# One PSUM bank per step in a Fourier mixing and gated feed-forward kernel: P, then Q added onto it

## The chip, the cores and the metric

The kernel runs on one core of one Trainium2 chip. The metric is the device time of one execution in microseconds (us). A profile of one execution gives, for every engine, when each instruction ran. The engines are TensorE (PE in the views, its weight loads PEld), VectorE (DVE), ScalarE (ACT), GpSimd (POOL) and SyncE (SP), which starts the transfers. Each engine works through its own list of instructions in order[...], so what an engine does late holds up everything behind it in its list. TensorE writes its results to PSUM[...]; the other engines read them from there.

## The reference, cut to what matters

```python
def _attn_ref(x):                       # x: (8, 3008, 256) float32
    X = np.fft.fft(x, axis=1)
    X = np.fft.fft(X, axis=2)
    return X.real

def _moe_ref(x, w_in, w_out):           # x: (24064, 256), w_in: (256, 2048), w_out: (2048, 256)
    h = x @ w_in
    g = h * (1.0 / (1.0 + np.exp(-1.702 * h)))
    return g @ w_out
```

A two-dimensional Fourier transform (its real part) of eight batches is followed by a feed-forward layer: a product, a sigmoid-gated activation, a product.

## The kernel before

The kernel uses symmetries of the real part. The last stage of the transform along the 256 columns is folded into `w_in`, and two rows of the input of the feed-forward layer come from the same two products, called P and Q here: one row has the hidden values P + Q, its mirror row P - Q + N, where N is a correction of rank one (`nb` times a column of `af2`).

The work is cut into 384 steps: 8 batches x 3 blocks x 2 halves x 8 pairs of 128 hidden features (`p`). Eight consecutive steps with the same block and half form a group; they add their output products onto the same banks. A step has 256 columns, in one of the six groups of each batch 225.

In every step the two products P and Q go into one bank each, `pa` and `pb`. ScalarE copies P to SBUF, VectorE makes P + Q, N - Q and P - Q + N (this last one in reversed order of columns), and one activation runs over both halves of `h`:

```python
def hidden(t):
    ...
    pa, pb = bank("pa"), bank("pb")                  # from a ring of four banks
    for ps, cs in ((pa, 0), (pb, 1)):
        for i in range(2):
            f = 2 * p + i
            halves(ps[:, i * 256:i * 256 + n], wcs[cs][:, f * 128:(f + 1) * 128], pq[:, cs, ks], start=True, stop=True)
    v = sp.tile([128, 512], F32, tag="v", name="v")
    nc.scalar.copy(two(v[:], n), two(pa[:], n))

def rows(t):
    ...
    nc.vector.tensor_tensor(two(h[:], n), two(v[:], n), two(pb[:], n), op=ALU.add)
    for i in range(2):
        f = 2 * p + i
        nc.vector.scalar_tensor_tensor(dif[:, i * 256:i * 256 + n], nb[:, ks], af2[:, f:f + 1],
                                       pb[:, i * 256:i * 256 + n], op0=ALU.mult, op1=ALU.subtract)
    ...                                              # h (second half, reversed) = pa + dif
def activate(t):
    g = free(ht[t][:], 0, [256, 4], [1, width(blk, hh)])
    nc.scalar.activation(g, g, ACTF.Gelu_apprx_sigmoid)
```

`halves` issues every product as two matmuls with 64 columns of weights each; each appears in the profile as two matmuls. A step thus has 8 x 2 matmuls for P and Q and, for the output, 7 x 2 x 2 = 28: the second product is done with a scheme of seven products in place of eight (Strassen's, in Winograd's form), except in the first eight steps. Its sums of `h` are made by GpSimd (`s1`, `s3`) and VectorE (`s2`, `s4`) in `sums`, and `product(t)` adds the seven products onto four banks. After the eighth step of a group `combine` puts the seven sums together on VectorE, transposes them and starts the stores:

```python
def combine(t):                                      # n columns; nothing unless p is the last
    ...
    for out_, i0, i1, how in ((u2, c1, m6, ALU.add), (c11, c1, m2, ALU.add), (u3, u2, m7, ALU.add),
                              (u2, u2, m5, ALU.add), (c12, u2, m3, ALU.add), (c22, u3, m5, ALU.add),
                              (c21, u3, m4, ALU.subtract)):
        nc.vector.tensor_tensor(out_, i0, i1, op=how)
    ...
    for half in range(2):
        turned(half, c[:, 2 * half:])                # one transpose of 128 x 512, then the stores
```

The main loop, with the order in which each engine gets its work:

```python
    for t in range(n + LAG):                         # LAG = 3
        if t < n:
            hidden(t)
        ...
        if t >= LAG:
            product(t - LAG)
        ...
        if 0 < t <= n:
            activate(t - 1)
            sums(t - 1, nc.gpsimd)
        sums(t - 2, nc.vector)
        if t < n:
            rows(t)
        if t >= LAG:
            combine(t - LAG)
        for fn, args in extra.get(t, ()):            # work of the next batch and block
            fn(*args)
```

The work in `extra` is the transform of the next batch and block: `fold1` on GpSimd (eight pieces, in every second step from the 7th of a batch on), `mix1` (16 products and two copies by ScalarE, in the steps 10, 14, 18 and 22 of a batch; in the first batch three steps later), `stage2` (products and four transposes by VectorE, in the steps 8, 24 and 40 of a batch).

Of the kernel before, what the change touches and what calls it, by code (L numbers as in the profile page):

```python
# [27 lines left out]
F32 = mybir.dt.float32  # L28
# [83 lines left out]
def kernel(ctx: ExitStack, tc, x, w_in, w_out, tab1, tab2, out):  # L112
# [13 lines left out]
    sp = ctx.enter_context(tc.tile_pool(name="sp", bufs=2, space=SB))  # L126
    op = ctx.enter_context(tc.tile_pool(name="op", bufs=2, space=SB))
    cv = ctx.enter_context(tc.tile_pool(name="cv", bufs=1, space=SB))
    psm = ctx.enter_context(tc.tile_pool(name="psm", bufs=4, space=PS))
    pso = ctx.enter_context(tc.tile_pool(name="pso", bufs=1, space=PS))  # L130
    ctx.enter_context(tc.manual_schedule())

    Xr = [nc.dram_tensor(f"Xr{b}", (NA, NJ, D), F32, kind="Internal").ap() for b in range(B)]
# [16 lines left out]

        return w[rows, jj * NM:jj * NM + 64]

    def bank(name):
        return psm.tile([128, 512], F32, tag="mm", name=name)

# [299 lines left out]

    NP = NF // 2
    steps = [(b, blk, hh, p) for b in range(B) for blk in range(NBLK) for hh in range(2) for p in range(NP)]
    vb, ht, st, pot, ot = {}, {}, {}, {}, {}  # L460

    def width(blk, hh):

        return 225 if (blk, hh) == (0, 1) else 256

    def two(ap, n):
        return free(ap, 0, [256, 2], [1, n])

    def halves(out, lhs, rhs, **how):
        for c0 in (0, 64):  # L470
            nc.tensor.matmul(out[c0:c0 + 64], lhsT=lhs[:, c0:c0 + 64], rhs=rhs, **how)  # L471

    def hidden(t):

        b, blk, hh, p = steps[t]
        n = width(blk, hh)
        pq, ks = pqt[b, blk], slice(hh * 256, hh * 256 + n)
        pa, pb = bank("pa"), bank("pb")
        for ps, cs in ((pa, 0), (pb, 1)):
            for i in range(2):  # L480
                f = 2 * p + i
                halves(ps[:, i * 256:i * 256 + n], wcs[cs][:, f * 128:(f + 1) * 128], pq[:, cs, ks], start=True, stop=True)
        v = sp.tile([128, 512], F32, tag="v", name="v")

        nc.scalar.copy(two(v[:], n), two(pa[:], n))  # L485
        vb[t] = v, pa, pb

    def rows(t):
        b, blk, hh, p = steps[t]
        n = width(blk, hh)  # L490
        nb, ks = nbt[b, blk], slice(hh * 256, hh * 256 + n)
        v, pa, pb = vb.pop(t)
        h = ht[t] = hp.tile([128, 2, 2, 256], F32, tag="h", name="h")
        dif = sp.tile([128, 512], F32, tag="dif", name="dif")
        nc.vector.tensor_tensor(two(h[:], n), two(v[:], n), two(pb[:], n), op=ALU.add)  # L495
        for i in range(2):
            f = 2 * p + i
            nc.vector.scalar_tensor_tensor(dif[:, i * 256:i * 256 + n], nb[:, ks], af2[:, f:f + 1],  # L498
                                           pb[:, i * 256:i * 256 + n], op0=ALU.mult, op1=ALU.subtract)

        full, rest = divmod(n, RUN)
        for at, blocks, m in ((0, full, RUN), (full * RUN, 1, rest)):
            if m:
                ins = [free(x[:], at, [256, 2], [RUN, blocks], [1, m]) for x in (pa, dif)]
                nc.vector.tensor_tensor(free(h[:], 512 + at + m - 1, [256, 2], [RUN, blocks], [-1, m]), *ins, op=ALU.add)  # L505

    def activate(t):
        b, blk, hh, p = steps[t]
        g = free(ht[t][:], 0, [256, 4], [1, width(blk, hh)])
        nc.scalar.activation(g, g, ACTF.Gelu_apprx_sigmoid)  # L510

    def sums(t, eng):

        if not NP <= t < len(steps):
            return
        h, n = ht[t], width(*steps[t][1:3])
        a11, a12, a21, a22 = h[:, 0, 0, :n], h[:, 0, 1, :n], h[:, 1, 0, :n], h[:, 1, 1, :n]
        if eng is nc.gpsimd:
            st[t] = sp.tile([128, 4, 256], F32, tag="s", bufs=3, name="s")
        s1, s2, s3, s4 = (st[t][:, q, :n] for q in range(4))  # L520
        if eng is nc.gpsimd:
            eng.tensor_tensor(s1, a21, a22, op=ALU.add)  # L522
            eng.tensor_tensor(s3, a11, a21, op=ALU.subtract)  # L523
        else:
            eng.tensor_tensor(s2, s1, a11, op=ALU.subtract)  # L525
            eng.tensor_tensor(s4, a12, s2, op=ALU.subtract)  # L526

    def product(t):

        b, blk, hh, p = steps[t]  # L530
        n = width(blk, hh)
        if p == 0:
            for q in range(4):
                pot[q] = pso.tile([128, 2, 256], F32, tag=f"o{q}", name=f"po{q}")
        h = ht.pop(t)
        if t < NP:

            plan = [(half, dh, wo[:, p, 2 * f + dh, :], h[:, half, f, :n], f)
                    for half in range(2) for dh in range(2) for f in range(2)]
        else:  # L540
            s = st.pop(t)
            plan = ((0, 0, wo[:, p, 0, :], h[:, 0, 0, :n], 0), (0, 1, wt[:, p, 1, :], s[:, 1, :n], 0),
                    (1, 0, wo[:, p, 2, :], h[:, 0, 1, :n], 0), (1, 1, wt[:, p, 2, :], s[:, 2, :n], 0),
                    (2, 0, wt[:, p, 0, :], s[:, 0, :n], 0), (2, 1, wo[:, p, 3, :], s[:, 3, :n], 0),
                    (3, 0, wt[:, p, 3, :], h[:, 1, 1, :n], 0))

        if t == len(steps) - 2:
            pot["plan"] = plan
            return
        if t == len(steps) - 1:  # L550
            plan = [it for two_ in zip(pot.pop("plan"), plan) for it in two_]

        for q, i, lhs, rhs, f in plan:
            halves(pot[q][:, i, :n], lhs, rhs, start=(p == 0 and i == 0 and f == 0), stop=(p == NP - 1), skip_group_check=True)
        if p < NP - 1 or t < NP:
            return
        c1 = pot["c"] = op.tile([128, 256], F32, tag="u0", bufs=1, name="u0")
        nc.scalar.copy(c1[:, :n], pot[0][:, 0, :n])  # L558

    def combine(t):  # L560

        b, blk, hh, p = steps[t]
        if p < NP - 1:
            return
        n = width(blk, hh)
        o = op.tile([128, 4, 256], F32, tag="os", name="os")

        def turned(half, src):

            nc.vector.transpose(free(o[:], half * 512, [32, 2], [64, 8], [1, 32]), free(src, 0, [256, 2], [32, 8], [1, 32]))  # L570
            store(b, blk, hh, o, half)

        if t < NP:
            for half in range(2):
                turned(half, pot[half][:])
            return
        c = cv.tile([128, 4, 256], F32, tag="m", bufs=2, name="c")
        if n < 256:
            nc.gpsimd.memset(c[:, :, n:], 0.0)
        (_, m6), (m2, m7), (m5, m3), (m4, _) = ((pot[q][:, 0, :n], pot[q][:, 1, :n]) for q in range(4))  # L580
        u2, u3 = (op.tile([128, 256], F32, tag=f"u{q}", bufs=1, name=f"u{q}")[:, :n] for q in (1, 2))
        c1 = pot["c"][:, :n]
        c11, c12, c21, c22 = (c[:, q, :n] for q in range(4))
        for out_, i0, i1, how in ((u2, c1, m6, ALU.add), (c11, c1, m2, ALU.add), (u3, u2, m7, ALU.add),
                                  (u2, u2, m5, ALU.add), (c12, u2, m3, ALU.add), (c22, u3, m5, ALU.add),
                                  (c21, u3, m4, ALU.subtract)):
            nc.vector.tensor_tensor(out_, i0, i1, op=how)  # L587
            if t == len(steps) - 1:
                if out_ is c12:
                    turned(0, c[:])  # L590
                elif out_ is c22 or out_ is c21:
                    i = int(out_ is c22)
                    nc.vector.transpose(free(o[:], 512 + 32 * i, [64, 8], [1, 32]), free(c[:], (2 + i) * 256, [32, 8], [1, 32]))
        if t == len(steps) - 1:
            store(b, blk, hh, o, 1)
            return
        for half in range(2):
            turned(half, c[:, 2 * half:])

    def store(b, blk, hh, o, half):  # L600

# [118 lines left out]
    def at(t, fn, *args):  # L720
        extra.setdefault(t, []).append((fn, args))
# [16 lines left out]
    at(4, rotate, 0, 4, NG)  # L738
    for i in range(NCK):
        at(7 + i, differences, i)  # L740
    for b in range(B):
        t0 = b * NBLK * NF
        late = 0 if b else 3
# [16 lines left out]
                at(t0 + blk * NF + 12, nyquist, *nxt)  # L760

    for t in range(n + LAG):
        if t < n:
            hidden(t)
        if t == 0:
            low_up(in2)
            nyquist(0, 0)
            low_down(in2)
        if t in rows_at:
            first_row(rows_at[t])  # L770
        if t >= LAG:
            product(t - LAG)
        if t in early:
            fold_w(early[t])

        if 0 < t <= n:
            activate(t - 1)
            sums(t - 1, nc.gpsimd)
        sums(t - 2, nc.vector)
        if t < n:  # L780
            rows(t)
        if t >= LAG:
            combine(t - LAG)
        for fn, args in extra.get(t, ()):
            fn(*args)

# [27 lines left out]
```

## Time and profile before

| | us |
|---|---|
| median of three runs | 1920.59 (1920.14 to 1921.92) |
| span of the profiled execution | 1919.2 |
| PE busy | 1907.5 (99%) |
| PEld busy | 1284.4 (67%) |
| DVE busy | 1409.3 (73%) |
| ACT busy | 674.7 (35%) |
| POOL busy | 768.2 (40%) |

The first part of the profile page gives the busy time of each engine as a share of the span. Matmuls overlap one another, so that a busy PE alone does not tell that it works at its peak; for that one looks at the distance between the starts of its instructions in the timeline. The groups give, for the instructions of one line and shape, their count, their busy time, the mean duration of one, and the idle time of the engine just before them with what ended it. The chain of waits follows the last instruction back to what released it, again and again, and gives shares of the span by engine.

### The profile page before, as it was taken

To read this page: it belongs to the slowest core of one execution; us is meant where nothing else is said; L and a number is where in the kernel's file an instruction comes from. 1 tells how busy PE (TensorE), PEld (TensorE's weight loads), DVE (VectorE), ACT (ScalarE), POOL (GpSimd) and SP (SyncE) were. 2 spreads that over 40 slices of the span, in tenths; PEclk is the share of its full clock that TensorE was granted. 3 is DMA by queue.
4 is the path that set the end of the run, shared out by engine and by line. 5 is a ranking of instruction groups with operands and counts; after the bars stand their busy time and mean duration, and the time that the engine had idled before them with its cause. 6 is when DMAs were issued, how large, how long until landed. Compare 5 with 4: busy or idle time off the path is not lost.

```text
span 1919.2 us, 46708 instructions
## 1 busy us (share of the span) xinstructions
PE 1907.5 (99%) x19184; PEld 1284.4 (67%) x19184; DVE 1409.3 (73%) x2937; ACT 674.7 (35%) x932; POOL 768.2 (40%) x1057
## 2 busy tenths in 40 slices
PE   9999999999999999999999999999999999999998
PEld 6676666766666666666667666676666766667665
DVE  7777777776787677767777677677777777778766
ACT  6533333333333333333333333333333333333332
POOL 4474324632256223552235523264323642223222
PEclk9999999999999999999999999999999999999999
DMA  8621630345212542126222272122820223202201
GB/s 282 163 52 37 115 34 12 60 62 99 18 22 51 99 61 25 48 33 103 41 29 50 44 107 33 16 51 44 126 18 13 18 53 53 18 13 28 18 12 23
DMA packets 145380, 104.66 MB, mean 55 GB/s; under 512 B 104914, under 2 KB 127986, under 8 KB 143984
## 3 DMA queue, kind: packets, MB, share of 16 engines
q1 hardware_dynamic: 143952, 101.14, 31.2%
q8 instruction: 153, 2.51, 0.6%
q10 hardware_dynamic: 1216, 0.52, 0.1%
q14 instruction: 59, 0.48, 0.1%
HBM read 58.38 MB, written 48.01 MB: 55 GB/s over the span
## 4 chain that ended last, share of the span: by engine, by line
PE 98%; DMA 1%; ACT 0%; DVE 0%; issue 0%; SPq 0%; ACTq 0%
PE po L471 59%; PE pa L471 17%; PE pb L471 17%; PE ps L226 2%; PE ps L328 1%; PE ps L279 1%; PE warm L297 1%; DMA raw<-in_moe_w_out_dram 0%; PE psw L444 0%; DMA t<-Td 0%; PE psr L314 0%; PE psf L454 0%; DMA Td<-e 0%; ACT h L510 0%; ACT r L384 0%
## 5 line engine op out<-in xcount | busy, mean ns | idle before, releaser
L471 PE MATMUL po<-s,wo 128*64 128x256 f32 (+1 forms) x6016 | 763.6, 375 | 0.0
L522 POOL TENSOR_TENSOR s<-h 128x256 f32<-128x256 f32 (+1 forms) x376 | 271.4, 722 | 1080.9 <-ACT h L510 1021.2
L471 PE MATMUL po<-h,wo 128*64 128x256 f32 (+1 forms) x4768 | 697.1, 375 | 0.0
L485 ACT COPY v<-pa 128x512 f32<-128x512 f32 (+1 forms) x384 | 222.1, 578 | 1061.3 <-PE pa L471 1061.3
L471 PEld LDWEIGHTS po<-s,wo 128*64 128x64 f32 x6016 | 433.0, 137 | 203.0
L495 DVE TENSOR_TENSOR h<-v,pb 128x512 f32<-128x512 f32 (+1 forms) x384 | 258.9, 674 | 405.3 <-PE pb L471 393.7
L471 PEld LDWEIGHTS po<-h,wo 128*64 128x64 f32 x4768 | 343.0, 137 | 161.2
L510 ACT ACTIVATE h<-h 128x1024 f32<-128x1024 f32 (+1 forms) x384 | 401.1, 1045 | 19.3 <-DVE h L505 17.0
L471 PE MATMUL pa<-pq,wcs 128*64 128x256 f32 (+1 forms) x3072 | 393.5, 377 | 1.9 <-ACT h L510 1.7
L471 PE MATMUL pb<-pq,wcs 128*64 128x256 f32 (+1 forms) x3072 | 390.3, 375 | 0.0
L498 DVE SCALAR_TENSOR_TENSOR dif<-nb,af,pb 128x256 f32<-128x256 f32 (+1 forms) x768 | 328.1, 468 | 0.9 <-ACT nb L346 0.9
L471 PEld LDWEIGHTS pa<-pq,wcs 128*64 128x64 f32 x3072 | 215.5, 137 | 115.9 <-issue 16.1
L471 PEld LDWEIGHTS pb<-pq,wcs 128*64 128x64 f32 x3072 | 221.2, 137 | 103.7 <-ACT xt L229 0.2
L523 POOL TENSOR_TENSOR s<-h 128x256 f32<-128x256 f32 (+1 forms) x376 | 277.1, 737 | 0.0
L505 DVE TENSOR_TENSOR h<-pa,dif 128x512 f32<-128x512 f32 (+1 forms) x448 | 265.4, 604 | 13.2
L526 DVE TENSOR_TENSOR s<-h,s 128x256 f32<-128x256 f32 (+1 forms) x376 | 192.0, 511 | 12.9
L525 DVE TENSOR_TENSOR s<-s,h 128x256 f32<-128x256 f32 (+1 forms) x376 | 180.8, 481 | 4.3 <-POOL s L522 4.3
L199 POOL TENSOR_TENSOR xt<-xt 111x510 f32<-111x510 f32 x56 | 74.6, 1332 | 4.4
L587 DVE TENSOR_TENSOR c<-u,po 128x256 f32<-128x256 f32 (+1 forms) x188 | 69.4, 409 | 2.5 <-PE po L471 0.9
L334 DVE STREAM_TRANSPOSE pq<-ps 128x256 f32<-128x256 f32 x96 | 34.6, 417 | 46.9 <-PE ps L328 46.9
L587 DVE TENSOR_TENSOR u<-u,po 128x256 f32<-128x256 f32 (+1 forms) x141 | 57.6, 409 | 8.3 <-ACT u L558 2.5
L570 DVE STREAM_TRANSPOSE os<-c 128x512 f32<-128x512 f32 x93 | 60.3, 686 | 0.0
(73 smaller groups left out, 516.0 us busy)
## 6 DMA issues: line engine op xcount, KB each, us to landing
out_dram<-os SPq DMA_DIRECT2D x284, 64.0 KB
Td<-xt SPq DMA_DIRECT2D x14, 768.0 KB
t<-Td SPq DMA_DIRECT2D x7, 1536.0 KB
xt<-in_x_dram SPq DMA_DIRECT2D x14, 512.0 KB
xt<-Xr SPq DMA_DIRECT2D x14, 512.0 KB
nb<-pq SPq DMA_DIRECT2D x23, 256.0 KB
out_dram<-os SPq DMA_DIRECT2D x96, 56.0 KB
Xr<-in_x_dram SPq DMA_DIRECT2D x7, 752.0 KB
```

The source lines that it names most:

```text
L199: eng.tensor_tensor(low, low, free(t, up + D - 1, [-D, 2], [-1, D - 1]), op=ALU.add)
L471: nc.tensor.matmul(out[c0:c0 + 64], lhsT=lhs[:, c0:c0 + 64], rhs=rhs, **how)
L485: nc.scalar.copy(two(v[:], n), two(pa[:], n))
L495: nc.vector.tensor_tensor(two(h[:], n), two(v[:], n), two(pb[:], n), op=ALU.add)
L498: nc.vector.scalar_tensor_tensor(dif[:, i * 256:i * 256 + n], nb[:, ks], af2[:, f:f + 1], pb[:, i * 256:i * 256 + n], op0=ALU.mult, op1=AL ...
L505: nc.vector.tensor_tensor(free(h[:], 512 + at + m - 1, [256, 2], [RUN, blocks], [-1, m]), *ins, op=ALU.add)
L510: nc.scalar.activation(g, g, ACTF.Gelu_apprx_sigmoid)
L522: eng.tensor_tensor(s1, a21, a22, op=ALU.add)
L523: eng.tensor_tensor(s3, a11, a21, op=ALU.subtract)
L525: eng.tensor_tensor(s2, s1, a11, op=ALU.subtract)
L526: eng.tensor_tensor(s4, a12, s2, op=ALU.subtract)
L587: nc.vector.tensor_tensor(out_, i0, i1, op=how)
```

## The change

What it does, in each step from the 9th on:

- **One bank.** P is put into a bank `x` (`begin`), one step ahead of its use. Later Q is added onto it in the same bank (`second`), so that the bank holds P + Q. Two banks are used in turn.
- **2P + N in SBUF.** Between `begin` and `second` VectorE reads the bank while it holds P alone, and writes 2P + N to SBUF (`doubled`). N was put there by ScalarE (`middle`, two steps ahead).
- **Activation from the bank.** ScalarE applies the activation to P + Q straight from the bank (`forward`). VectorE subtracts the bank from 2P + N, which gives P - Q + N, reversed (`backward`), and ScalarE activates that half in SBUF (`activate_back`).
- **Order.** TensorE's step becomes: Q of this step, the first two of the seven products, P of the next step, the other five products. The seven products have other places in the banks; one of them has a bank of its own.
- GpSimd's sums of a step now come in the same step's turn as its activation, in place of the next one's.

It frees two PSUM banks and takes VectorE work away, which is room for a second level of the seven-product scheme. The code of that level is in the change too, but it is switched off (`deep` returns `False` for every step); of it only `small_weights` runs, 16 small sums by GpSimd in the steps 9 to 12, whose results nobody reads. The narrow groups get 226 columns in place of 225.

The diff, cut to its core:

```diff
-    psm = ctx.enter_context(tc.tile_pool(name="psm", bufs=4, space=PS))
-    pso = ctx.enter_context(tc.tile_pool(name="pso", bufs=1, space=PS))
+    psp = ctx.enter_context(tc.tile_pool(name="psp", bufs=1, space=PS))
...
-        return 225 if (blk, hh) == (0, 1) else 256
+        return 226 if steps[t][1:3] == (0, 1) else 256
...
+    def begin(t):
+        n = width(t)
+        x = xb[t] = bank("x", f"b{t % 2}")
+        for i in range(2):
+            halves(x[:, i * 256:i * 256 + n], *operands(t, 0, i), start=(i == 0), stop=False)
+
+    def second(t):
+        n = width(t)
+        for i in range(2):
+            halves(xb[t][:, i * 256:i * 256 + n], *operands(t, 1, i), start=False, stop=True)
+
+    def middle(t):
...
+            nc.scalar.activation(g[:, i * 256:i * 256 + n], nbt[b, blk][:, hh * 256:hh * 256 + n], ACTF.Copy,
+                                 scale=af2[:, f:f + 1])
+
+    def doubled(t):
+        n = width(t)
+        g = two(gt[t][:], n)
+        nc.vector.scalar_tensor_tensor(g, two(xb[t][:], n), 2.0, g, op0=ALU.mult, op1=ALU.add)
+
+    def forward(t):
...
+        nc.scalar.activation(two(h[:], n), two(xb[t][:], n), ACTF.Gelu_apprx_sigmoid)
+
+    def backward(t):
+        reversed_sum(t, gt.pop(t), xb.pop(t), ALU.subtract)
+
+    def activate_back(t):
+        g = free(ht[t][:], 512, [256, 2], [1, width(t)])
         nc.scalar.activation(g, g, ACTF.Gelu_apprx_sigmoid)
...
+    def deep(t):
+        return False
...
+            plan = [(0, 0, wo[:, p, 0, :], h[:, 0, 0, :n]), (0, 1, wt[:, p, 1, :], s[:, 1, :n]),
+                    (1, 0, wt[:, p, 2, :], s[:, 2, :n]), (1, 1, wt[:, p, 0, :], s[:, 0, :n]),
+                    (2, 0, wo[:, p, 3, :], s[:, 3, :n])]
+            if not deep(t):
+                plan += [(2, 1, wo[:, p, 2, :], h[:, 0, 1, :n]), (5, 0, wt[:, p, 3, :], h[:, 1, 1, :n])]
+        todo = plan[:2] if part == 0 else plan[2:]
...
+        m2, m4 = pot[2][:, 256:256 + n], pot[5][:, 0:n]
+        plan = [*plan[:1], (c11, c1, m2, ALU.add), plan[1], plan[2], plan[4], plan[3], (c21, u3, m4, ALU.subtract)]
...
     for t in range(n + LAG):
-        if t < n:
+        if t < NP:
             hidden(t)
...                                  # the first eight steps as before; at the end of the eighth:
+            if t == NP - 1:
+                for ahead in range(2):
+                    middle(NP + ahead)
+                begin(NP)
+        else:
+            if t < n:
+                if t + 2 < n:
+                    middle(t + 2)
+                second(t)
+            product(t - LAG, 0)
+            if t + 1 < n:
+                begin(t + 1)
+            product(t - LAG, 1)
...
+            if t < n:
+                forward(t)
+            sums(t - 2, nc.vector)
+            if t < n:
+                backward(t)
+                activate_back(t)
+                sums(t, nc.gpsimd)
+        if NP <= t + 1 < n:
+            doubled(t + 1)
...
         if t >= LAG:
             combine(t - LAG)
...
+        if t >= NP:
+            spare[:] = ["b2", f"b{t % 2}"]           # the banks of mix1 and stage2
```

The copy `c1` of the first of the seven sums, which ScalarE made at the end of `product`, is now made at the start of `combine`; the order of the seven sums in `combine` is as before.

## The prediction

> **What bounds the kernel now.** I read the page's first part, then the chain of waits, then TensorE's timeline. The first part has TensorE busy for 99% of the span, VectorE for 73%; the chain that ended last says the same:
>
> ```profile
> PE 1907.5 (99%) x19184; PEld 1284.4 (67%) x19184; DVE 1409.3 (73%) x2937; ACT 674.7 (35%) x932; POOL 768.2 (40%) x1057
> ...
> PE 98%; DMA 1%; ACT 0%; DVE 0%; issue 0%; SPq 0%; ACTq 0%
> ```
>
> Busy alone does not show that nothing is lost, so I take one step from TensorE's timeline (columns: start us, duration us, engine, line, operation, out<-in, count):
>
> ```profile
> 965.61 1.03 PE L471 MATMUL pa<-pq,wcs 128*64 128x256 f32 x8
> 966.48 1.03 PE L471 MATMUL pb<-pq,wcs 128*64 128x256 f32 x8
> 967.34 0.60 PE L471 MATMUL po<-h,wo 128*64 128x256 f32 x4
> ...
> 970.36 1.03 PE L471 MATMUL pa<-pq,wcs 128*64 128x256 f32 x8
> ```
>
> A step lasts 970.36 - 965.61 = **4.75 us** for 44 matmuls, 0.108 us each; eight take 0.865 us (966.48 - 965.61), and their results are usable 1.14 us after the first start (ScalarE's copy of this `pa` starts at 966.75), which is 0.28 us after the last issue slot. A narrow step lasts 4.18 us. So TensorE issues without a gap, and only fewer matmuls could make it quicker.
>
> VectorE's timeline over a `combine` shows how large the bursts are that TensorE does not feel today:
>
> ```profile
> 993.48 0.41 DVE L587 TENSOR_TENSOR u<-u,po 128x256 f32<-128x256 f32 x1
> 993.81 0.41 DVE L587 TENSOR_TENSOR c<-u,po 128x256 f32<-128x256 f32 x1
> ...
> 996.11 1.30 DVE L570 STREAM_TRANSPOSE os<-c 128x512 f32<-128x512 f32 x2
> 997.34 0.59 DVE L525 TENSOR_TENSOR s<-s,h 128x256 f32<-128x256 f32 x1
> ...
> 1000.21 0.69 DVE L505 TENSOR_TENSOR h<-pa,dif 128x512 f32<-128x512 f32 x1
> 1000.82 0.41 DVE L525 TENSOR_TENSOR s<-s,h 128x256 f32<-128x256 f32 x1
> 1001.26 0.43 DVE L526 TENSOR_TENSOR s<-h,s 128x256 f32<-128x256 f32 x1
> 1001.61 0.68 DVE L495 TENSOR_TENSOR h<-v,pb 128x512 f32<-128x512 f32 x1
> ```
>
> From the second sum to the transposes 2.30 us pass, the transposes hold VectorE 1.23 us, the two `s` sums 0.44 + 0.35 us where GpSimd is quiet, the reversed sum 0.61 us (start to start; neighbours overlap a little). In all, `combine` costs 3.86 us, and afterwards VectorE is behind. Nothing waits, since `pa`/`pb` rotate over four banks and `s` is used a whole step later.
>
> [...] the first `s` sum takes 0.41 us alone, 1.41 us at 1027.78 beside GpSimd's fold. [...]
>
> **The change part by part.**
>
> *TensorE's work* is the same: 16 matmuls for P and Q, 28 for the output. Adding Q onto P saves no matmul. The 64 narrow steps get a column more[...].
>
> *VectorE's work* falls: gone are the sum over `v,pb` (0.674 us mean) and the two for `dif` (2 x 0.468); new is `doubled`, for which I take 0.70 us: 0.43 us for a 256-wide scalar_tensor_tensor where undisturbed (a pair lasts 0.86) plus 0.27 us for 256 more columns (tensor_tensor: 0.685 us at 512, 0.414 at 256). That is 0.9 us off each of 376 steps, but VectorE ends no wait of TensorE today: **worth 0**. ScalarE goes from 0.58 + 1.05 us to four operations of together about 2 us in 4.75: **0**.
>
> *The new wait.* Before, TensorE's next P and Q needed only a free bank. Now Q of a step may not start before VectorE has read P alone. In a wide step, counted from the start of `second`: Q 0 to 0.86; two products to 1.73; P of the next step to 2.59, usable at 2.87; five products to 4.75. VectorE: two `s` sums from 0; the bank is complete at 1.14; `forward` 0.59 us; `backward` from about 1.8 to 2.4; `doubled` 2.87 to 3.57. Restarting TensorE costs about 0.3 us more (0.1 for the semaphore as seen between other engines here, 0.2 from a weight load's start to its matmul), so it may go at 3.9, needed at 4.75. **An ordinary step fits, with 0.9 us to spare.**
>
> *A step with `combine`.* It comes in VectorE's list after `doubled`, so it delays the next step's. Its second sum needs the sixth of the seven products, issued by 4.32, usable at 4.60. Then, by the intervals above: + 2.30 to the transposes (6.90), + 1.23 (8.13), + 0.80 for the `s` sums (8.93), + 0.60 `backward` (9.53), + 0.70 `doubled` (10.23), + 0.3 restart = 10.5. TensorE would want it at 2 x 4.75 = 9.50: **it stands 1.0 us**. The next step recovers fully, as there the P read is the ordinary case.
>
> There are 46 such combines (48 groups; the first has only two transposes, the last nothing after it). In batches 2 to 7, two each (steps 10 and 18) fall together with `mix1`, whose 1.03 us of matmuls push the need out. Of these 12 the wide six then cost nothing, the narrow six, by the same sums with 4.18 us steps and a VectorE that does not shrink as much, 0.6 us: 3.6. The narrow one of the last batch has no `mix1`: 1.6. The other 33: 33 x 1.0 = 33. **Together +38 us.**
>
> *`stage2`.* Its second bank is that of `x`, so P of the step after next waits for its four transposes (1.37 us to the next start). By the intervals it is late by 0.1 us in wide steps and 0.3 in narrow ones: 15 x 0.1 + 8 x 0.3 = **+4 us**.
>
> *Start and end.* At the change of schemes `begin`, `doubled` and `second` stand back to back, once: about 1.2 us. GpSimd has its backlog there: it is busy without a break from 99.5 to 115.8 us, and gets 16 more sums, some 0.4 us each by its rates (256 columns 0.73), 6 us that can hold VectorE's `s` sums and the first `mix1`: I put 3. In the last `combine` the second sum waits for a later product than before: 1. **Together +5 us.**
>
> Sum: 1.2 + 38 + 4 + 5 = 48; 1920.6 + 48 = **1969 us**, 2.5% more.
>
> **The rivals.**
>
> *Hidden after all:* VectorE has 0.9 us less per step and catches up within the burst, so that TensorE's wait vanishes; 1922 to 1930 us. For it speaks that VectorE's load falls by 330 us in sum. Against it: the saved work lies in the steps around, while the burst of 3.9 us plus 2.1 us of in-order work must fit between the sixth product and a `second` 4.9 us later.
>
> *Waits in ordinary steps too:* if ScalarE's lists or GpSimd's folds (up to 1.4 us in one `s` sum) delay `backward`, so that 0.9 us does not suffice, a few tenths in some 100 of the steps with folds or `mix1` add 20 to 40 us: 1990 to 2010. For it speaks the 1.41 us; against it that these sums stand at the start of the step, where VectorE would wait for the bank anyway until 1.8, and that the operations reading PSUM kept their durations beside GpSimd.
>
> *A gain:* fewer VectorE reads might ease something in the first 100 us, where TensorE idles 5.5 us; but those steps keep the old scheme. Under 3 us.
>
> **Range and chances.** The stall is a difference of two sums of ten intervals, each good to some 5%; 0.5 us either way is 17 us over 33 combines. Down to 0.4 us each gives about 1945; 1.5 us each, or the second rival in part, gives 1985 to 2000. I choose 1945 to 2000. The 2% line is 1959, which the stalls reach at 0.7 us each: 0.67 for slower, 0.31 for within 2%, 0.02 for faster.
>
> **What the profile after would show.** PE's busy share falls by 2 to 3 points. TensorE's ordinary step is still 4.75 us; its gap sits before the Q matmuls two steps behind each eighth product, about 1 us, released by VectorE's `g<-x,g`, and is missing where `mix1` lies. VectorE's busy time falls by about 300 us, ScalarE's rises by about 130. Wrong would be: no gaps there (the burst hides), gaps in ordinary steps (second rival), matmuls that start further apart than 0.108 us when they alternate banks or add onto P, or a wait of GpSimd or ScalarE as the usual releaser.

## The result, and the profile after

The changed kernel takes 2043.9 us (median of four runs, 2043.04 to 2048.42) against 1920.66 us before (four runs): a ratio of 1.0645, 95% interval 1.0627 to 1.0664. That is 123 us more, where 48 were predicted, and outside the range.

The first part of the page and the chain of waits, of the changed kernel (in the chain, a name ending in q is an engine's sequencer, and "issue" is time in which an engine waited for nothing that the profile shows):

```profile
PE 1944.1 (95%) x19184; PEld 1295.6 (63%) x19184; DVE 1267.6 (62%) x2185; ACT 847.7 (42%) x1684; POOL 811.8 (40%) x1073
...
PE 65%; DMA 15%; DVE 11%; SPq 3%; ACT 2%; issue 2%; POOL 1%; DVEq 0%; ACTq 0%; POOLq 0%
```

TensorE has the same 19184 matmuls but now idles for 5% of a longer span, and the chain holds 15% of transfers where it had 1%. The view of who waited for whom names the transfer (columns: us in total, times, longest us):

```profile
ACT g L542 <- DMA nb<-pq: 145.4, 22, 10.0
...
PEld x L478 <- DVE g L548: 72.1, 51, 6.0
...
PE x L478 <- DVE g L548: 49.1, 51, 5.6
```

TensorE waits for VectorE's `g<-x,g` (`doubled`), as predicted; but ScalarE waits for `nb`, the broadcast row of the correction N, in 22 places. One of them, in the timelines of SyncE, ScalarE, VectorE and TensorE (start us, duration us, and in brackets the idle time before with its releaser):

```profile
1108.65 0.94 SPq L346 DMA_DIRECT2D nb<-pq  x1
```

```profile
1110.91 0.58 ACT L562 ACTIVATE h<-h 128x452 f32<-128x452 f32 x1 [0.76 <-DVE h L503]
1120.26 0.91 ACT L542 ACTIVATE g<-nb,af 128x256 f32<-128x256 f32 x2 [8.76 <-DMA nb<-pq]
1121.07 0.53 ACT L555 ACTIVATE h<-x 128x452 f32<-128x452 f32 x1
```

```profile
1121.63 0.69 DVE L503 TENSOR_TENSOR h<-g,x 128x448 f32<-128x448 f32 x2 [8.36 <-ACT h L555]
1122.24 0.62 DVE L548 SCALAR_TENSOR_TENSOR g<-x,g 128x452 f32<-128x452 f32 x1
```

```profile
1117.13 0.65 PE L230 MATMUL ps<-xt,w 47*64 47x256 f32 x4
1122.47 1.97 PE L230 MATMUL ps<-xt,w 47*64 47x256 f32 x12 [4.69 <-DVE h L503]
1124.37 1.77 PE L478 MATMUL x<-pq,wcs 128*64 128x226 f32 x8
```

The reader can follow the fall of the dominoes. The transfer is issued at 1108.65. ScalarE could begin `middle` for the first step of the next block at about 1111.5 (1120.26 less 8.76), two steps before that step. The row is there only at 1120.26, 11.6 us after its issue. Behind `middle` in ScalarE's list stands `forward` of the *current* step, which needs no `nb` at all; behind it, on VectorE, `backward` and `doubled`; TensorE needs the bank that `backward` frees (here for the products `ps` of `mix1`, elsewhere for Q). All this work stands still for one row of a later block.

Before, the same transfer was issued at the same place, and no engine waited for it. SyncE's and VectorE's timelines of the kernel before:

```profile
1043.01 0.76 SPq L342 DMA_DIRECT2D nb<-pq  x1
```

```profile
1059.00 0.87 DVE L498 SCALAR_TENSOR_TENSOR dif<-nb,af,pb 128x256 f32<-128x256 f32 x2
```

There were 16.0 us from issue to first use. The change left 2.9 us (1108.65 to 1111.5), because N is now made two steps ahead of its step, and VectorE's use came in the middle of a step while ScalarE's comes at its start.

### The profile page after: what moved, and what is told of

Its sections match the earlier page's. It is cut to its first block, busy times and chain, and to the rows that moved or that the text cites. A ratio compares the mean times of both kernels' runs of the same rounds, so it can differ in the third digit from the quotient of the medians.

```text
span 2041.2 us, 45270 instructions
## 1 busy us (share of the span) xinstructions
PE 1944.1 (95%) x19184; PEld 1295.6 (63%) x19184; DVE 1267.6 (62%) x2185; ACT 847.7 (42%) x1684; POOL 811.8 (40%) x1073
## 4 chain that ended last, share of the span: by engine, by line
PE 65%; DMA 15%; DVE 11%; SPq 3%; ACT 2%; issue 2%; POOL 1%; DVEq 0%; ACTq 0%; POOLq 0%
PE po L478 38%; PE x L478 23%; DMA nb<-pq 11%; DVE os L677 2%; DVE c L709 2%; DVE h L503 2%; SPq L769 2%; PE ps L230 1%; DVE u L709 1%; PE ps L332 1%; DVE g L548 1%; DMA xt<-in_x_dram 1%; DMA t<-Td 1%; DMA xt<-Xr 1%; DVE s L578 1%
## 5 line engine op out<-in xcount | busy, mean ns | idle before, releaser
L478 PE MATMUL x<-pq,wcs 128*64 128x256 f32 (+1 forms) x6016 | 780.7, 381 | 49.1 <-DVE g L548 49.1
L478 PEld LDWEIGHTS x<-pq,wcs 128*64 128x64 f32 x6016 | 428.1, 138 | 282.2 <-DVE g L548 72.1
L478 PE MATMUL po<-s,wo 128*64 128x256 f32 (+1 forms) x4512 | 575.6, 376 | 0.0
L503 DVE TENSOR_TENSOR h<-g,x 128x512 f32<-128x512 f32 (+2 forms) x440 | 258.1, 599 | 506.7 <-ACT h L555 506.2
L555 ACT ACTIVATE h<-x 128x512 f32<-128x512 f32 (+1 forms) x376 | 220.8, 587 | 551.8 <-PE x L478 516.1
L542 ACT ACTIVATE g<-nb,af 128x256 f32<-128x256 f32 (+1 forms) x752 | 333.7, 492 | 146.2 <-DMA nb<-pq 145.4
L562 ACT ACTIVATE h<-h 128x512 f32<-128x512 f32 (+1 forms) x376 | 233.8, 622 | 376.5 <-DVE h L503 376.5
L548 DVE SCALAR_TENSOR_TENSOR g<-x,g 128x512 f32<-128x512 f32 (+1 forms) x376 | 255.3, 679 | 108.5 <-PE x L478 108.4
L574 POOL TENSOR_TENSOR held<-h 128x256 f32<-128x256 f32 (+1 forms) x94 | 68.6, 730 | 374.8 <-ACT h L562 366.9
L478 PE MATMUL po<-held,wo 128*64 128x256 f32 (+1 forms) x1504 | 192.1, 375 | 0.0
L575 POOL TENSOR_TENSOR held<-h 128x256 f32<-128x256 f32 (+1 forms) x94 | 82.7, 880 | 0.0
```

The costliest lines, as they stand in the source:

```text
L542: nc.scalar.activation(g[:, i * 256:i * 256 + n], nbt[b, blk][:, hh * 256:hh * 256 + n], ACTF.Copy, scale=af2[:, f:f + 1])
L548: nc.vector.scalar_tensor_tensor(g, two(xb[t][:], n), 2.0, g, op0=ALU.mult, op1=ALU.add)
L555: nc.scalar.activation(two(h[:], n), two(xb[t][:], n), ACTF.Gelu_apprx_sigmoid)
```

## The experiments

**1. The broadcast earlier.** Only its place in the program moves:

```diff
-                at(t0 + blk * NF + 12, nyquist, *nxt)
+                at(t0 + blk * NF + 9, nyquist, *nxt)
```

> The changed kernel, with the broadcast of the correction row (nb) issued three steps earlier (step 9 of a block in place of 12), nothing else. Theory A: the new cost is mostly that ScalarE now needs nb two steps ahead (in middle), stands in its in-order list for the transfer (145 us in 22 waits, landing some 11.5 us after issue) and so holds up the activation from the bank, VectorE and TensorE. TensorE's visible gaps after those waits sum to 60 us, the restarts add 0.25 us each and eight stretches at half clock some 2 us each, about 83 us: so 1961 us (1950 to 1970), no ScalarE wait on nb over 1 us. Theory B: the in-order burst of combine on VectorE, or matmuls that add onto P, make the loss and ScalarE's waits only overlap with it: 2030 us or more.

1958.98 us, ratio to before 1.0198 (1.0183 to 1.0214). 85 us of the 123 are gone, and with them every wait of ScalarE for `nb`. TensorE's waits for `doubled` are now

```profile
PE x L478 <- DVE g L548: 16.0, 35, 0.9
```

in place of 49.1 us in 51. The cause of the larger part is shown; what remains is 38 us. The 85 us are more than the waits: TensorE stood idle 60 us longer in the changed kernel (97.1 us of the span, here 37.1), and it was busy 24 us longer with the same matmuls (1944.1 us, here 1920.5), for the most part because they ran slower after long stops (last section; the mean granted clock of the profiled execution was 0.985 there and is 0.996 here).

**2. The broadcast later**, step 13 in place of 12:

> The changed kernel with the broadcast of nb issued one step later (13 in place of 12). Theory A: each of 22 waits grows by a step of 4.75 us or 4.2 us, all of it passed on: some 100 us more, about 2140 us (2120 to 2160). Theory B: less than 10 us more.

2068.75 us (two runs): 25 us more, not 100. Neither number of that expectation is right, and SyncE's timeline tells why (first the changed kernel, then this one):

```profile
1101.38 4.85 SPq L769 DMA_DIRECT2D out_dram<-os  x12
1106.28 1.54 SPq L171 DMA_DIRECT2D Xr<-in_x_dram  x2
1107.87 0.68 SPq L173 DMA_DIRECT2D Xr<-in_x_dram  x1
1108.65 0.94 SPq L346 DMA_DIRECT2D nb<-pq  x1
```

```profile
1117.82 4.84 SPq L769 DMA_DIRECT2D out_dram<-os  x12
1122.71 1.54 SPq L171 DMA_DIRECT2D Xr<-in_x_dram  x2
1124.29 0.68 SPq L173 DMA_DIRECT2D Xr<-in_x_dram  x1
1125.07 0.85 SPq L346 DMA_DIRECT2D nb<-pq  x1
```

The issue still follows the same transfers at once: SyncE does not keep time with the steps, it works off a list. For this block nothing stands between the places 12 and 13, so nothing moved (ScalarE waits 8.67 us where it waited 8.76). Only in the second block of a batch does another transfer (the fill of the next batch) lie in between. In the third batch the row then came 13.2 us after its issue in place of 11.6, and TensorE's gap grew from 1.28 to 3.33 us. In sum TensorE's idle time grew by 10 us only (97.1 to 106.9); for the other 17 us it was busy longer with the same matmuls (1944.1 and 1961.4 us, at a mean granted clock of 0.985 and 0.976). It also corrects the reading of run 1: what helped there was to stand ahead of the stores of step 10, which put the issue 20 us ahead of the first use (1051.44 and 1071.80).

**3. The kernel before with a later broadcast**, step 14 in place of 12:

> The kernel before, with its broadcast of nb issued two steps later (14 in place of 12), so that VectorE's first use comes as soon after the issue as ScalarE's in the changed kernel. Theory A with slack: VectorE waits some 3 to 9 us for nb at each of 23 blocks, but four banks for P and Q and three steps to the output products let TensorE go on: under 15 us more, 1920 to 1935 us. If the wait alone decides and the structure has no part in it: some 80 us more, about 2000 us.

1920.95 us, ratio 1.0001 (0.9992 to 1.0009). By the same finding this is no test of the slack: in no block did the issue move by two steps (all 23 lie within 2 us of those before). That the kernel before had slack rests on its trace (16.0 us), not on this run.

**4. N one step ahead in place of two**, with the broadcast as in the change:

```diff
-                    for ahead in range(2):
-                        middle(NP + ahead)
+                    middle(NP)
...
-                if t + 2 < n:
-                    middle(t + 2)
+                if t + 1 < n:
+                    middle(t + 1)
```

> The changed kernel, nb issued at step 12 as there, but ScalarE makes N (middle) one step ahead of its use in place of two. Theory A: what costs is how soon ScalarE's list comes to nb; a step later takes 4.2 to 4.75 us off each of the 22 waits (4.7 to 10 us), so that 14 of them go to 0 to 2 us and are absorbed, the 8 longest to 4 to 5.5 us, which TensorE feels by up to 1 us each: 1960 to 1970 us. Theory B (the transfer is late in itself, whoever waits for it): within 15 us of 2044.

1965.73 us, ratio 1.0240 (1.0224 to 1.0255), as the first theory had it. ScalarE's waits for `nb` fall to

```profile
ACT g L542 <- DMA nb<-pq: 21.2, 17, 4.7
```

from 145.4 us in 22. The transfer itself is not changed here; what costs is how early ScalarE's list comes to it. The waits that are left go with 7 us more than in run 1, which has none.

**5. A shorter burst.** On top of run 1 the two transposes of `combine` go one step later, behind `doubled`:

```diff
-        for half in range(2):
-            turned(t, o, half, c[:, 2 * half:])
+        pot["wait"] = t, o, c
...
             doubled(t + 1)
+        transposes()                     # of the combine of the step before
```

> The changed kernel with nb issued at step 9, and the two transposes and stores of a combine put one step later on VectorE, after the next doubled. Theory A: the trace shows 34 gaps of 0.43 us idle before Q's matmuls two steps behind a group's last product, with restart 0.65 us each; 1.2 us less in the burst takes them all away: 22 us less than with the early nb alone, about 1939 us. If what remains has nothing to do with the burst: within 3 us of the kernel with the early nb alone.

1936.01 us, ratio 1.0077 (1.0062 to 1.0092): 23 us less than run 1. After 127 us TensorE never idles between two matmuls any more until its last one. The burst of `combine` is shown as the cause of this part.

**6. Without the sums that nobody reads**, on top of run 5:

```diff
-        at(9 + i, small_weights, i)
```

> As the kernel with the early nb and the late transposes, without the 16 sums of small_weights, which nobody reads. Theory A: they stand in GpSimd's list before the fold for the second batch, and hold up its first mix1, at which TensorE idles 5.94 us at 126.9 us; without them that gap closes: 6 to 8 us less, about 1929 us (1926 to 1932). If the gap comes from elsewhere: within 1 us of 1936. No step here does fewer matmuls than the kernel before, so it can't fall below 1920.

1928.22 us, ratio 1.0036 (1.0024 to 1.0049): 7.8 us less. The gap of 5.94 us before the second batch's first `mix1` is closed. Two stretches of this kernel (from and to in us, length, busy time and instructions of TensorE, its weight loads, VectorE, ScalarE and GpSimd, granted clock, share and rate of transfers):

```profile
0.00:100.00 100.00, 90.12 (x712) 57.83 (x714) 68.90 (x102) 59.88 (x89) 45.79 (x46) 1.00 0.74 213
...
400.00:1840.00 1440.00, 1440.00 (x14684) 984.06 (x14682) 957.52 (x1655) 626.87 (x1272) 581.41 (x777) 1.00 0.31 46
```

From 400 to 1840 us TensorE is never idle, as before. Where the last 7.6 us lie is told by the matmuls of `stage2`: their second turn starts at 96.51 us (before: 90.91), 5.6 us late, the third 6.2 us late, and from then on each batch adds 0.22 us, near the 0.15 us that the added column of its eight narrow steps comes to. That is an estimate from the steps before: 4.75 us with 256 columns and 4.18 with 225 give 0.57 / 31 = 0.018 us a column, and 64 such steps give the 1.2 us in the prediction's sum. Of the 5.6 us, 3.1 stand already at the eighth step (P at 83.73, before 80.66), which keeps the old scheme; their cause stays open.

**7. The second level switched on.** The change makes room for it, so I switched it on, on top of run 5:

```diff
-        return False
+        return NP <= t < last
```

> As the kernel with the early nb and the late transposes, with the second level of the seven-product scheme switched on for all groups but the first and the last (deep). Two products of 256 columns in each of two steps become 14 matmuls of 128 columns: 28 x (128 / 256 x 0.108 us) = 1.51 us for 16 x 0.108 = 1.73 us, 0.22 us in two steps, 184 times, about 40 us if TensorE stays the bound: 1895 to 1905 us. If VectorE's added sums (four of some 0.4 us in two steps, and in combine) or weight loads stand in the way: 1920 to 1950 us.

2046.31 us, ratio 1.0653 (1.0638 to 1.0667). Two steps now take 9.30 us of matmuls in place of 9.50 (starts at 799.74 and 809.04), near the estimate, but the loss is far larger than the rival allowed. TensorE's timeline, twice in each group:

```profile
829.28 1.08 PE L478 MATMUL x<-pq,wcs 128*64 128x256 f32 x8 [1.47 <-DVE g L548]
...
835.13 1.08 PE L478 MATMUL x<-pq,wcs 128*64 128x256 f32 x8 [1.09 <-DVE g L548]
```

**8. Its combine spread out**: the last sum and transpose a step later, second level from the third group on, `small_weights` in steps 16 to 19.

> As the kernel with the second level switched on, but the last part of a deep group's combine (one sum, one transpose) a step later, the second level only from the third group on, and small_weights in steps 16 to 19. There TensorE stood twice per group, 1.47 and 1.09 us idle (0.25 us more each with the restart), 46 times, about 140 us, each time for VectorE. Theory A (VectorE's burst): 1.1 us less in the step of the second stall takes most of it: 46 x 1.1 = 50 us, and 6 us at the start: about 1990 us (1975 to 2000). If the second level's small matmuls or weight loads cost: within 15 us of 2046.

1990.0 us (two runs), as the burst theory had it.

**9. Half of the second level's sums on GpSimd**, on top of run 8:

```diff
-            nc.vector.tensor_tensor(out, i0, i1, op=how)
+            (nc.vector if part else nc.gpsimd).tensor_tensor(out, i0, i1, op=how)
```

> As the split one, with half of the second level's sums of h (two of four) made by GpSimd in place of VectorE: some 0.8 to 1.2 us less for VectorE in every second step, 1.46 us more for GpSimd there. Theory A: VectorE's bursts then fit and TensorE's saved matmuls show: 1900 to 1925 us, TensorE idle on VectorE under 20 us in all. If GpSimd's folds and sums now come too late[...]: 1940 us or more.

1958.04 us, ratio 1.0186 (1.0169 to 1.0203): 32 us better, but the first number is missed by far. The second (1940 us or more) is met, but run 10 shows another reason than the one given with it. 49 us of TensorE's waits are left. ScalarE's timeline ahead of one of them:

```profile
826.50 0.27 ACT L736 COPY held<-po 128x128 f32<-128x128 f32 x1 [0.61 <-PE po L623]
828.24 0.40 ACT L747 COPY u<-held 64x256 f32<-64x256 f32 x1 [1.48 <-DVE held L746]
828.68 0.40 ACT L748 COPY held<-held 64x256 f32<-64x256 f32 x1
829.09 0.40 ACT L749 COPY u<-held 64x256 f32<-64x256 f32 x1
829.51 0.86 ACT L542 ACTIVATE g<-nb,af 128x226 f32<-128x226 f32 x2
830.27 0.53 ACT L555 ACTIVATE h<-x 128x452 f32<-128x452 f32 x1
```

The pattern of `nb` again: copies of `combine_small` wait in ScalarE's list for VectorE's sums, and the next `forward`, which has nothing to do with them, comes behind.

**10. The order mended**, on top of run 9: the sums of `combine_small` first in the step after, ScalarE's copies behind that step's activations, and the rest of combine a step later again.

> As the kernel with the second level partly on GpSimd, where TensorE still stands 44 times, 1.05 us idle (1.3 with the restart), two steps behind a group's last product: in its trace ScalarE's copies in combine_small wait for VectorE's sums (66 us in 45 waits) and stand in ScalarE's list ahead of the next activation from the bank. Here the sums come first in the step after, and ScalarE's copies behind that step's activations. Theory A (the place in ScalarE's in-order list, as with nb): 44 x 1.3 = 57 us less, 1901 us (1895 to 1912), faster than the kernel before. Theory B (VectorE's amount of work in these steps): the 1.6 us of sums ahead of the step's other work only shift the gap, 1940 us or more.

1908.79 us, ratio 0.9937 (0.9924 to 0.9951): 0.6% faster than the kernel before. 49 us came from the place of the instructions alone. The same engine, the same place in the program, with `forward` (L555) now ahead of the copies:

```profile
807.70 0.54 ACT L555 ACTIVATE h<-x 128x452 f32<-128x452 f32 x1
810.95 0.58 ACT L562 ACTIVATE h<-h 128x452 f32<-128x452 f32 x1 [2.71 <-DVE h L503]
811.55 0.40 ACT L756 COPY u<-held 64x256 f32<-64x256 f32 x1
```

TensorE is busy for 99% of the span again. The time lies in the expected range, 8 us above the 1901: 0.56 us of idle are left in one step of the batches 2 to 7 each, and 2.7 us ahead of two `mix1` for the second batch (0.42 and 2.30); where the rest lies stays open.

## Why the prediction was wrong

- **What bounds the kernel, same matmuls at the same pace:** right. Ordinary steps take 4.75 us after the change too (starts at 1149.10 and 1153.85).
- **VectorE's and ScalarE's work, "ScalarE goes from 0.58 + 1.05 us to four operations of together about 2 us in 4.75: 0":** this is the step that failed. I compared the amounts of work (ScalarE's busy time did rise, by 173 us, to 42%) and not what each new operation waits for. `middle` brought a transfer into ScalarE's list, two steps earlier than its old reader. Run 1 puts 85 us on it, run 4 shows that the place in the list matters. The list of what must be ready, and since when, was in the diff and in the transfers' issues of the kernel before; I had not set them against each other. A second size was off without cost: VectorE's busy time fell by 142 us (1409.3 to 1267.6), not by some 300, because its `s` and `held` sums rose from 0.50 to 0.69 us in the mean. Those beside GpSimd's sums are the long ones (0.74 us at 1104.19, against 0.40 at 1102.26, where GpSimd is quiet); in run 6, where TensorE no longer idles in these steps, VectorE's busy time is about the same (1278.9 us).
- **"An ordinary step fits, with 0.9 us to spare":** right, save behind `nb`; between those stretches TensorE has no gap but those of `combine`. That `backward` starts only behind `forward`, which the estimate took as given, the changed kernel's trace shows: VectorE waited for ScalarE there 299 times, 506.2 us in sum (at 1150.81, 0.03 us after `forward` ended).
- **A step with `combine`, 1.0 us, 34 times and six more of 0.6:** the mechanism is right, the size too large. The kernel of run 1, free of the waits for `nb`, shows gaps of 0.43 us in the four wide groups of a batch and none where `mix1` lies (0.6 had been put for the narrow ones there). By VectorE's timeline of the changed kernel and, below it, TensorE's:

```profile
733.40 0.42 DVE L709 TENSOR_TENSOR c<-u,po 128x256 f32<-128x256 f32 x1 [0.71 <-PE po L478]
...
735.64 1.30 DVE L677 STREAM_TRANSPOSE os<-c 128x512 f32<-128x512 f32 x2
736.87 0.38 DVE L577 TENSOR_TENSOR s<-s,h 128x256 f32<-128x256 f32 x1
...
738.22 0.68 DVE L548 SCALAR_TENSOR_TENSOR g<-x,g 128x512 f32<-128x512 f32 x1
```

```profile
728.87 1.03 PE L478 MATMUL x<-pq,wcs 128*64 128x256 f32 x8
...
738.96 1.08 PE L478 MATMUL x<-pq,wcs 128*64 128x256 f32 x8 [0.43 <-DVE g L548]
```

  Counted from the step's start at 728.87, `doubled` ends 10.03 us later (predicted 10.23), and TensorE starts 0.06 us after that, not 0.3: of the 0.44 us too much, 0.24 lie in the restart and 0.20 in the chain ahead of it. It stands 738.96 - 728.87 - 9.50 = 0.59 us; 34 x 0.59 = 20 us, and run 5 took 23 away. Predicted were 38.
- **`stage2`, 4 us:** did not come. In run 6 its starts fall behind those before by only the 0.22 us a batch named there.
- **Start, 5 us:** `small_weights` cost 7.8, where 3 stood for it.
- **In sum:** 85 (not foreseen) + 23 (38) + 7.8 (3) + 7.6 for the rest (7) = 123. That the rest fits is luck: 4 us of `stage2` that did not come stand against a slower beginning that was not foreseen. Without the omission the steps would have given 1959, inside the range, but with a combine too dear and a start too cheap.
- **Rivals:** "hidden after all" fell with run 1, whose gaps of `combine` are still there, and run 5, which closes them. The second rival named ScalarE's lists, but for tenths in steps with folds, not for a transfer. What stood against it, that operations reading PSUM keep their durations beside GpSimd, has its numbers in the trace of before: `h<-pa,dif` took 0.69 us at 1021.03, beside the fold, and 0.69 us at 1031.35, where GpSimd is quiet.

## What to carry to other kernels

When an operation moves to another engine or an earlier step, list for each of its inputs when it becomes ready and when it is now first asked for; the amount of work says nothing of it. An instruction in an in-order list that waits for something nobody needs yet also stops everything behind it, so put work for later behind work for now (here worth 85 us once and 49 us a second time). And a bank that is read between two of its writes makes every burst on the reading engine a matter of that one step: spread the burst, as in run 5 (23 us).

## What the runs showed of the hardware

In these runs a step number moved a transfer only where something else stood between the two places in the issuing engine's list (with nothing between, ScalarE waited 8.67 us in run 2 where it had waited 8.76, and all 23 issues of run 3 lay within 2 us of those before). TensorE's restart was cheaper than I took it to be: 0.06 us after the releasing operation's end (738.90 to 738.96). And long stops cost beyond their length: in the changed kernel, after the idle 4.69 us above, eight matmuls took 1.77 us where narrow ones take 0.93, and the granted clock from 1122 to 1125 us was 0.50; after 2.94 us of idle at 1207.51 eight wide ones took 1.08, and the clock from 1207 to 1212 us was 1.00. The traces give no clean limit. In run 2, after two stops of 3.21 us each, half pace came at once in one case (the eight wide matmuls at 1479.01 took 1.98) and some 2 us later in the other (eight at 975.00 took 1.08, eight at 977.36 took 1.92). In the changed kernel it also came after a stop of only 1.95 us (before 1617.08): soon after it, at 1618.09, eight narrow ones took 1.42, and the clock from 1618 to 1622 us was 0.57.
